# Query projection and output projection of a cached attention block: from TensorE to VectorE multiply-adds

## The chip, the cores and the metric

The kernel runs on one core of a Trainium2 chip. The metric is the device time in microseconds of one execution. The kernel before takes 1057.88 us, the median of three runs (1057.36 to 1058.01). A second number is used throughout: the span of one profiled execution, from its first instruction to its last. PE is TensorE, PEld its weight loads, DVE is VectorE, ACT is ScalarE, POOL is GpSimd, and SP is the engine whose queue issues all loads.

## The reference

One token passes through a transformer block whose keys and values are cached. Everything is fp32, the width is D = 640, and there are H = 32 heads of size 192 over 8192 cached positions.

```python
sa, ca, ga, sb, cb, gb = split6(silu(c) @ w_mod)        # w_mod: 640 x 3840
h = layernorm(x) * (1 + ca) + sa
q = (h @ wq).reshape(32 heads, 192)                      # wq: 640 x 6144
s = einsum("hd,hkd->hk", q, k_cache) * 192 ** -0.5       # k_cache: 32 x 8192 x 192
o = einsum("hk,hkd->hd", softmax(s), v_cache)            # v_cache: 32 x 8192 x 192
x = x + ga * (o.reshape(6144) @ wo)                      # wo: 6144 x 640
h = layernorm(x) * (1 + cb) + sb
x = x + gb * (relu(h @ w1 + b1) ** 2 @ w2 + b2)          # w1: 640 x 1536, w2: 1536 x 640
```

The two caches are 6144 KB a head each, 403 MB in all, and every byte is read once.

## The kernel before, in words

**Loads and slots.** Three large buffers ("slots") take turns. All loads go through SP's queue, in the order of the program: wm0 (w_mod for sa and ca, wq of the first pair, and the small vectors), k of head 0, v of head 0, k of head 1, v of head 1, and so on. A load waits on SP until the slot that it reuses is free; a load queued behind it waits too. The slot of k of a head is free when the last operation that reads it has ended (the reductions at the end of `keys`, and whatever reads the weights that came along), and it is then refilled with v of the next head. The slot of v is free when `values` has ended, and is refilled with a later k.

Heads are taken in pairs i = h // 2, and the weights of a pair ride along with k: the load of an even head brings the part of wq that makes the query of the next pair, that of an odd head the part of wo for the pair before. Heads 1 and 30 bring none. The load of k of head 30 is cut in two and that of head 31 in four pieces; the last piece of head 31 holds the rows of wo. After head 31's k come wm1 (wo of the last pair, and w_mod for ga; a second load brings sb and cb), v of head 31, w1 in two pieces, w_mod for gb, and w2 in five pieces, 3840 KB in all.

**One head.** `keys` (L192 to L208) works in place on the 64 positions of a partition, in two halves (head 31: four quarters). For each half VectorE multiplies k by the broadcast query (L201), GpSimd folds 7 of 16 parts of the products in half (L203), VectorE sums the rest (L204) and then GpSimd's share (L205). Behind the first half, `between(0)` is called: in an even head it is `query(i + 1)`, in an odd one `attend(i - 1)`. `softmax` finds the maximum over the partitions with one product of TensorE (L220) and takes the exponential on ScalarE (L228). `values` (L240) is 24 products of TensorE, 48 in the trace, which shows each fp32 product as two records. At the start of an odd head `project` (L254, L256, L258) normalises the pair before and leaves, by a product with `quad`, its outputs as columns in PSUM (ps_oT). The instructions of each engine run in the order in which the program lists them.

**query and attend.** The input h1 lies over the partitions: 4 groups of 32 lanes, and KB = 5 columns. hR is h1 with each column copied over 128 columns (L175). `query` makes five products (L181), each with a column block of hR as weights and 128 x 384 of wq as data, which add up in PSUM; ScalarE copies the sum to qb with the scale (L183). `attend` copies 96 columns of ps_oT to oT (L262), and makes six products (L267) that add up in one PSUM bank, att_a, over 15 pairs. `gather` runs in head 31 behind its third quarter's reductions: it copies att_a to SBUF and spreads it over the four groups of att (L280), to which the last pair adds its own products (L272) at the end.

**The end.** After head 31: project and attend of the last pair, the residual with ga, the second layernorm, the product with w1 (ps_f, L343), mod(5) for gb (L140), two rounds of products whose result is not used (ps_warm, L355), the product with w2 (ps_y, L363), the residual (L366, L367), and the store.

The program's order is fixed by hand: no scheduler moves instructions.

Of the kernel before, what the change touches and what calls it, by code (L numbers as in the profile page):

```python
# [20 lines left out]
DG = D // G  # L21
FG = FF // G
KB = DG // 32
FB = FG // 32
PW = 2 * DH
E = 8
ED = 64
NV = DH // ED
NPAIR = H // 2
# [16 lines left out]
def block_kernel(ctx: ExitStack, tc: tile.TileContext, kw, ky, vc, wm0, wm1, w1, gb, w2, out):  # L46
    nc = tc.nc
    const = ctx.enter_context(tc.tile_pool(name="const", bufs=1))
    strm = ctx.enter_context(tc.tile_pool(name="strm", bufs=3))
    work = ctx.enter_context(tc.tile_pool(name="work", bufs=2))  # L50
    psum = ctx.enter_context(tc.tile_pool(name="psum", bufs=1, space=bass.MemoryType.PSUM))
# [48 lines left out]
    def layernorm(x, copies, scale1, shift, name, between=lambda: None):  # L100

        n = x.shape[1]
        s = const.tile([P, 1], F32, name=name + "_s")
        nc.vector.tensor_reduce(s, x, axis=AX.X, op=ALU.add)
        m = const.tile([P, 1], F32, name=name + "_m")
        tm = total(s, name + "_tm")
        between()
        nc.vector.tensor_scalar(m, tm, 1.0 / (copies * D), None, op0=ALU.mult)
# [10 lines left out]
        nc.vector.scalar_tensor_tensor(h, xm, rs, scale1(), op0=ALU.mult, op1=ALU.mult)  # L119
        nc.vector.tensor_add(h, h, shift())  # L120
        return h
# [49 lines left out]
        return ca1  # L171

    h1 = layernorm(x_c, 1, scale_a, lambda: ma[:, :KB, 0], "ln1")
    hR = const.tile([P, KB, P], F32, name="hR")
    nc.vector.tensor_copy(hR, h1[:, :, None].to_broadcast([P, KB, P]))  # L175

    def query(i, w):
        w = w.rearrange("p (b n) -> p b n", b=KB)
        ps = psum.tile([P, 512], F32, tag="q", name=f"ps_q{i}", bufs=2)
        for b in range(KB):  # L180
            nc.tensor.matmul(ps[:, :PW], hR[:, b], w[:, b], start=(b == 0), stop=(b == KB - 1))  # L181
        qb_t[i] = work.tile([P, PW], F32, name=f"qb{i}", tag="qb")
        nc.scalar.activation(qb_t[i], ps[:, :PW], AF.Copy, scale=DH ** -0.5)  # L183


    att_a = psum.tile([P, 512], F32, tag="att", name="att_a")
# [56 lines left out]
    os_t = {}  # L243
# [14 lines left out]
        nc.tensor.matmul(os_t[i][:, :n], os_[:n].rearrange("p a d -> p (a d)"), quad[:n], start=True, stop=True)  # L258

    def attend(i, w):  # L260
        oT = work.tile([P, 96], F32, tag="oT", name=f"oT{i}")
        nc.vector.tensor_copy(oT, os_t.pop(i)[:, :96])  # L262
        w = w.rearrange("p (j n) -> p j n", j=3)
        if i + 1 < NPAIR:
            for j in range(3):
                for g in range(2):
                    nc.tensor.matmul(att_a[32 * g:32 * (g + 1), :2 * DG], oT[:, 32 * j:32 * (j + 1)],  # L267
                                     w[:, j, 2 * DG * g:2 * DG * (g + 1)], start=(i == 0 and j == 0), stop=(i == NPAIR - 2 and j == 2))
            return
        for j in range(3):  # L270
            for g in range(G):
                nc.tensor.matmul(att_t[0][32 * g:32 * (g + 1), :DG], oT[:, 32 * j:32 * (j + 1)],  # L272
                                 w[:, j, DG * g:DG * (g + 1)], start=False, stop=(j == 2))
# [67 lines left out]
    for b in range(KB):  # L341
        for g in range(G):
            nc.tensor.matmul(pf[32 * g:32 * (g + 1), :FG], hT2[:, b], w1_t[:, b, FG * g:FG * (g + 1)],  # L343
                             start=(b == 0), stop=(b == KB - 1))
    f = work.tile([P, FG], F32, name="f", tag="spread", bufs=1)
# [15 lines left out]
    for b in range(FB):  # L361
        for g in range(G):
            nc.tensor.matmul(py[32 * g:32 * (g + 1), :DG], fT[:, b], w2_t[:, b, DG * g:DG * (g + 1)],  # L363
                             start=(b == 0), stop=(b == FB - 1))
# [46 lines left out]
```

## Time and profile before

| what | value |
|---|---|
| time, median of three runs | 1057.88 us |
| span of the profiled execution | 1055.5 us |
| VectorE busy | 831.4 us (79%), 409 instructions |
| TensorE busy, matmuls | 463.7 us (44%), 2356 records |
| GpSimd busy | 194.8 us (18%) |
| ScalarE busy | 33.4 us (3%) |
| transfers of SP's queue | 451.83 MB, 99.3% of 16 engines' span |
| rate over the span | 428 GB/s |

The profiled execution has a time of its own only as this span; the medians are of other executions, and lie 2.4 us above it. A row of the timeline gives the start in the span, the duration, the engine, the line, the operation with what it writes and reads, the number of instructions, and in brackets how long the engine was idle before and what ended that. A row of the groups gives busy time and the mean duration in ns. A row of the stretches gives from and to, the length, the busy time of PE, PEld, DVE, ACT and POOL, then the granted clock of TensorE (1.00 is full), the share of the 16 transfer engines and the rate in GB/s.

### The profile page before, as it was taken

To read this page: it belongs to the slowest core of one execution; us is meant where nothing else is said; L and a number is where in the kernel's file an instruction comes from. 1 tells how busy PE (TensorE), PEld (TensorE's weight loads), DVE (VectorE), ACT (ScalarE), POOL (GpSimd) and SP (SyncE) were. 2 spreads that over 40 slices of the span, in tenths; PEclk is the share of its full clock that TensorE was granted. 3 is DMA by queue.
4 is the path that set the end of the run, shared out by engine and by line. 5 is a ranking of instruction groups with operands and counts; after the bars stand their busy time and mean duration, and the time that the engine had idled before them with its cause. 6 is when DMAs were issued, how large, how long until landed. Compare 5 with 4: busy or idle time off the path is not lost.

```text
span 1055.5 us, 5687 instructions
## 1 busy us (share of the span) xinstructions
PE 463.7 (44%) x2356; PEld 155.0 (15%) x2356; DVE 831.4 (79%) x409; ACT 33.4 (3%) x88; POOL 194.8 (18%) x72
## 2 busy tenths in 40 slices
PE   3234443355543345463334534335453335535446
PEld 1101111111111111120111111101111111111113
DVE  2886878978787987878888687997878798789963
ACT  1000000000000000000000000000000000000000
POOL 0211112211212221212221212221221221122110
PEclk9667666766666766666676666666666666767769
DMA  9999999999999999999999999999999999999997
GB/s 403 435 434 428 432 440 427 441 424 437 433 433 428 440 424 441 424 439 427 431 437 437 422 442 430 428 439 426 439 429 433 428 438 433 434 427 432 424 426 310
DMA packets 11410, 452.18 MB, mean 428 GB/s; under 512 B 1269, under 2 KB 1273, under 8 KB 1785
## 3 DMA queue, kind: packets, MB, share of 16 engines
q1 hardware_dynamic: 11384, 451.83, 99.3%
q8 instruction: 18, 0.29, 0.1%
q14 instruction: 8, 0.06, 0.0%
HBM read 451.82 MB, written 0.00 MB: 428 GB/s over the span
## 4 chain that ended last, share of the span: by engine, by line
DMA 42%; DVE 39%; PE 17%; ACT 1%; issue 1%; SPq 0%; DVEq 0%; ACTq 0%
DMA k<-in_kw 36%; DVE k L201 21%; PE ps_o L240 14%; DVE sc L204 12%; DVE sc L205 5%; DMA k<-in_ky 3%; DMA w_t<-in_w 2%; PE ps_mx L220 1%; DMA wm_t<-in_wm 1%; ACT p L228 1%; PE ps_sum L97 1%; PE ps_mod L140 1%; PE ps_q L181 1%; DVE nm L222 0%; DVE mp L218 0%
## 5 line engine op out<-in xcount | busy, mean ns | idle before, releaser
L201 DVE TENSOR_TENSOR k<-k,qb 128x6144 f32<-128x6144 f32 (+1 forms) x66 | 419.7, 6359 | 141.6 <-DMA k<-in_kw 134.4
L203 POOL TENSOR_TENSOR k<-k 128x1344 f32<-128x1344 f32 (+1 forms) x66 | 194.1, 2941 | 820.9 <-DVE k L201 476.1
L240 PE MATMUL ps_o<-v,p 128*32 128x512 f32 x1536 | 290.4, 731 | 17.2 <-ACT p L228 17.2
L204 DVE TENSOR_REDUCE sc<-k 128x18 f32<-128x3456 f32 (+1 forms) x66 | 240.5, 3644 | 4.3
L220 PE MATMUL ps_mx<-ident,mp 128*128 128x128 f32 x64 | 25.5, 501 | 416.2 <-DVE mp L218 416.2
L240 PEld LDWEIGHTS ps_o<-v,p 128*32 128x32 f32 x1536 | 68.4, 131 | 215.4 <-issue 193.1
L267 PE MATMUL att_a<-k,oT 128*32 128x320 f32 x180 | 49.6, 720 | 114.2 <-DVE oT L262 113.1
L205 DVE TENSOR_REDUCE sc<-k 128x14 f32<-128x1344 f32 (+1 forms) x66 | 99.0, 1500 | 0.0
L220 PEld LDWEIGHTS ps_mx<-ident,mp 128*128 128x128 f32 x64 | 16.1, 312 | 442.8 <-DVE mp L218 421.0
L181 PE MATMUL ps_q<-k,hR 128*128 128x384 f32 x150 | 52.3, 496 | 0.0
L228 ACT ACTIVATE p<-sc,nm 128x256 f32<-128x256 f32 x32 | 16.2, 508 | 760.6 <-DVE nm L222 496.9
L267 PEld LDWEIGHTS att_a<-k,oT 128*32 128x32 f32 x180 | 13.7, 161 | 136.7 <-DVE oT L262 116.7
L222 DVE TENSOR_REDUCE nm<-ps_mx 128x1 f32<-128x128 f32 x32 | 9.3, 291 | 28.5 <-PE ps_mx L220 28.5
L181 PEld LDWEIGHTS ps_q<-k,hR 128*128 128x128 f32 x150 | 27.3, 190 | 27.9 <-issue 11.7
L254 DVE SCALAR_TENSOR_TENSOR om<-ps_o,r,mask 96x512 f32<-96x512 f32 x32 | 23.9, 747 | 6.5 <-PE ps_o L240 5.4
L256 DVE TENSOR_REDUCE os<-om 96x64 f32<-96x512 f32 x32 | 21.8, 682 | 1.1
L140 PE MATMUL ps_mod<-wm_t,silu 128*32 128x320 f32 (+1 forms) x120 | 11.7, 550 | 14.6 <-DVE silu L128 14.6
L97 PE MATMUL ps_sum<-sp,ones 128*128 128x2 f32 x32 | 9.4, 364 | 17.2 <-ACT p L228 17.2
L183 ACT ACTIVATE qb<-ps_q 128x384 f32<-128x384 f32 x16 | 7.9, 491 | 195.2 <-PE ps_q L181 195.2
L97 PEld LDWEIGHTS ps_sum<-sp,ones 128*128 128x128 f32 x32 | 8.0, 312 | 21.9 <-ACT p L228 21.9
L145 DVE COPY mods<-ps_mod 128x320 f32<-128x320 f32 (+1 forms) x4 | 1.6, 398 | 10.2 <-PE ps_mod L140 10.2
L76 DVE COPY small<-wm_t 128x27 f32<-128x27 f32 x1 | 0.2, 179 | 11.2 <-DMA wm_t<-in_wm 11.2
(77 smaller groups left out, 90.9 us busy)
## 6 DMA issues: line engine op xcount, KB each, us to landing
k<-in_kw SPq DMA_DIRECT2D x29, 7104.0 KB, 27.4
v<-in_vc SPq DMA_DIRECT2D x32, 6144.0 KB, 22.1
k<-in_ky SPq DMA_DIRECT2D x1, 6144.0 KB, 28.3
k<-in_ky SPq DMA_DIRECT2D x2, 3072.0 KB, 21.5
k<-in_kw SPq DMA_DIRECT2D x3, 1536.0 KB, 15.5
wm_t<-in_wm SPq DMA_DIRECT2D x1, 4173.5 KB, 12.7
wm_t<-in_wm SPq DMA_DIRECT2D x1, 3200.0 KB, 29.3
wm_t<-in_wm SPq DMA_DIRECT2D x1, 2560.0 KB, 18.2
```

The source lines that it names most:

```text
L97: nc.tensor.matmul(ps[:, :n], ones, src, start=True, stop=True)
L140: nc.tensor.matmul(ps[32 * g:32 * (g + 1), :n * DG], e[:, b:b + 1].to_broadcast([P, 32]), wb[:, :, DG * g:DG * (g + 1)], start=(b == 0), s ...
L181: nc.tensor.matmul(ps[:, :PW], hR[:, b], w[:, b], start=(b == 0), stop=(b == KB - 1))
L201: nc.vector.tensor_mul(pr, pr, q[:, None, :].to_broadcast([P, n, DH]))
L203: nc.gpsimd.tensor_add(half, half, pr[:, m:, DH // 2:])
L204: nc.vector.tensor_reduce(s[:, :m], pr[:, :m], axis=AX.X, op=ALU.add)
L205: nc.vector.tensor_reduce(s[:, m:], half, axis=AX.X, op=ALU.add)
L220: nc.tensor.matmul(ps[:, :P], mp.to_broadcast([P, P]), ident, start=True, stop=True)
L228: nc.scalar.activation(p, sc[:, :, None].to_broadcast([P, NPOS, 32 // E]), AF.Exp, bias=nm, accum_out=sp[:, h % 2:h % 2 + 1])
L240: nc.tensor.matmul(ps_t[h][32 * g:32 * (g + 1)], p[:, E * j:E * (j + 1)].rearrange("p e r -> p (e r)"), t[:, j, g], start=(j == 0), stop=( ...
L254: nc.vector.scalar_tensor_tensor(om[:n], ps_t.pop(h)[:n].rearrange("p (d e) -> p d e", e=E), r2[:n, a:a + 1], mask[:n, None, :].to_broadca ...
L267: nc.tensor.matmul(att_a[32 * g:32 * (g + 1), :2 * DG], oT[:, 32 * j:32 * (j + 1)], w[:, j, 2 * DG * g:2 * DG * (g + 1)], start=(i == 0 an ...
```

## The change

`query` and `attend` use a new helper, `weighted`. It multiplies each block of a weight row by its own column scalar and adds the blocks up in SBUF, on VectorE: for wq five operations over 128 x 384 elements, for wo three over 128 x 640. What is left is a sum over the 128 partitions. For the query TensorE makes it at once, by one product with a matrix of ones. For wo the sum over 15 pairs is kept as rows in att_s, 128 x 640, and `gather` sums over the partitions once, by four products with columns of ones that put the result straight into att. oT holds three columns instead of 96 for these pairs, as one column per j is enough for a scalar. The last pair keeps its products on TensorE. hR, the bank att_a and the copy of it by ScalarE are gone. TensorE issues 154 products less (308 records). SP's loads, their order and their sizes are the same; the slots of k are read by VectorE and GpSimd only.

```diff
-    hR = const.tile([P, KB, P], F32, name="hR")
-    nc.vector.tensor_copy(hR, h1[:, :, None].to_broadcast([P, KB, P]))
+    def weighted(acc, w, by, first):
+        for j, c in enumerate(by):
+            if first and j == 0:
+                nc.vector.tensor_scalar(acc, w[:, j], c, None, op0=ALU.mult)
+            else:
+                nc.vector.scalar_tensor_tensor(acc, w[:, j], c, acc, op0=ALU.mult, op1=ALU.add)

     def query(i, w):
-        w = w.rearrange("p (b n) -> p b n", b=KB)
+        qp = work.tile([P, PW], F32, name=f"qp{i}", tag="qp", bufs=1)
+        weighted(qp, w.rearrange("p (b n) -> p b n", b=KB), [h1[:, b:b + 1] for b in range(KB)], True)
         ps = psum.tile([P, 512], F32, tag="q", name=f"ps_q{i}", bufs=2)
-        for b in range(KB):
-            nc.tensor.matmul(ps[:, :PW], hR[:, b], w[:, b], start=(b == 0), stop=(b == KB - 1))
+        nc.tensor.matmul(ps[:, :PW], ones, qp, start=True, stop=True)
...
-    att_s = const.tile([P, 2 * DG], F32, name="att_s")
-    nc.vector.memset(att_s, 0.0)
+    att_s = const.tile([P, D], F32, name="att_s")
...
         if i + 1 < NPAIR:
-            for j in range(3):
-                for g in range(2):
-                    nc.tensor.matmul(att_a[32 * g:32 * (g + 1), :2 * DG], oT[:, 32 * j:32 * (j + 1)],
-                                     w[:, j, 2 * DG * g:2 * DG * (g + 1)], start=(i == 0 and j == 0), stop=(i == NPAIR - 2 and j == 2))
+            oT = work.tile([P, NV], F32, tag="oT", name=f"oT{i}")
+            nc.vector.tensor_copy(oT, os_t.pop(i)[:, :32 * NV].rearrange("p (j r) -> p j r", j=NV)[:, :, 0])
+            weighted(att_s, w, [oT[:, j:j + 1] for j in range(NV)], i == 0)
             return
...
     def gather():
-        nc.scalar.activation(att_s[:64], att_a[:64, :2 * DG], AF.Copy)
         att_t.append(psum.tile([P, 512], F32, tag="o", name="att", bufs=3))
         for g in range(G):
-            nc.tensor.matmul(att_t[0][32 * g:32 * (g + 1), :DG], ident[:, 32 * (g // 2):32 * (g // 2) + 1].to_broadcast([P, 32]),
-                             att_s[:, DG * (g % 2):DG * (g % 2 + 1)], start=True, stop=False)
+            nc.tensor.matmul(att_t[0][32 * g:32 * (g + 1), :DG], ones[:, :32],
+                             att_s[:, DG * g:DG * (g + 1)], start=True, stop=False)
```

More of the change, by code (lines that the diff above doesn't have):

```diff
@@ L173, in block_kernel @@
     h1 = layernorm(x_c, 1, scale_a, lambda: ma[:, :KB, 0], "ln1")
-    hR = const.tile([P, KB, P], F32, name="hR")
-    nc.vector.tensor_copy(hR, h1[:, :, None].to_broadcast([P, KB, P]))
+    def weighted(acc, w, by, first):
[4 more added lines that the diff above has]
+                nc.vector.scalar_tensor_tensor(acc, w[:, j], c, acc, op0=ALU.mult, op1=ALU.add)
     def query(i, w):
-        w = w.rearrange("p (b n) -> p b n", b=KB)
+        qp = work.tile([P, PW], F32, name=f"qp{i}", tag="qp", bufs=1)
+        weighted(qp, w.rearrange("p (b n) -> p b n", b=KB), [h1[:, b:b + 1] for b in range(KB)], True)
         ps = psum.tile([P, 512], F32, tag="q", name=f"ps_q{i}", bufs=2)
-        for b in range(KB):
-            nc.tensor.matmul(ps[:, :PW], hR[:, b], w[:, b], start=(b == 0), stop=(b == KB - 1))
+        nc.tensor.matmul(ps[:, :PW], ones, qp, start=True, stop=True)
         qb_t[i] = work.tile([P, PW], F32, name=f"qb{i}", tag="qb")
         nc.scalar.activation(qb_t[i], ps[:, :PW], AF.Copy, scale=DH ** -0.5)
-    att_a = psum.tile([P, 512], F32, tag="att", name="att_a")
-    att_s = const.tile([P, 2 * DG], F32, name="att_s")
-    nc.vector.memset(att_s, 0.0)
+    att_s = const.tile([P, D], F32, name="att_s")
     att_t = []
@@ L260, in attend @@
     def attend(i, w):
-        oT = work.tile([P, 96], F32, tag="oT", name=f"oT{i}")
-        nc.vector.tensor_copy(oT, os_t.pop(i)[:, :96])
-        w = w.rearrange("p (j n) -> p j n", j=3)
+        w = w.rearrange("p (j n) -> p j n", j=NV)
         if i + 1 < NPAIR:
-            for j in range(3):
-                for g in range(2):
-                    nc.tensor.matmul(att_a[32 * g:32 * (g + 1), :2 * DG], oT[:, 32 * j:32 * (j + 1)],
-                                     w[:, j, 2 * DG * g:2 * DG * (g + 1)], start=(i == 0 and j == 0), stop=(i == NPAIR - 2 and j == 2))
+            oT = work.tile([P, NV], F32, tag="oT", name=f"oT{i}")
+            nc.vector.tensor_copy(oT, os_t.pop(i)[:, :32 * NV].rearrange("p (j r) -> p j r", j=NV)[:, :, 0])
+            weighted(att_s, w, [oT[:, j:j + 1] for j in range(NV)], i == 0)
             return
-        for j in range(3):
+        oT = work.tile([P, 32 * NV], F32, tag="oTl", name=f"oT{i}", bufs=1)
+        nc.vector.tensor_copy(oT, os_t.pop(i)[:, :32 * NV])
+        for j in range(NV):
             for g in range(G):
                 nc.tensor.matmul(att_t[0][32 * g:32 * (g + 1), :DG], oT[:, 32 * j:32 * (j + 1)],
-                                 w[:, j, DG * g:DG * (g + 1)], start=False, stop=(j == 2))
+                                 w[:, j, DG * g:DG * (g + 1)], start=False, stop=(j == NV - 1))
     def gather():
-        nc.scalar.activation(att_s[:64], att_a[:64, :2 * DG], AF.Copy)
         att_t.append(psum.tile([P, 512], F32, tag="o", name="att", bufs=3))
         for g in range(G):
-            nc.tensor.matmul(att_t[0][32 * g:32 * (g + 1), :DG], ident[:, 32 * (g // 2):32 * (g // 2) + 1].to_broadcast([P, 32]),
-                             att_s[:, DG * (g % 2):DG * (g % 2 + 1)], start=True, stop=False)
+            nc.tensor.matmul(att_t[0][32 * g:32 * (g + 1), :DG], ones[:, :32],
+                             att_s[:, DG * g:DG * (g + 1)], start=True, stop=False)
     x_t = spread(x_c, KB, "x_t")
```

## The prediction

> **What bounds the kernel now.** I read the page's queue table first, then the timeline of VectorE with what ended each idle stretch, then the chain that ended last.
>
> ```profile
> q1 hardware_dynamic: 11384, 451.83, 99.3%
> ```
>
> The transfer queue is busy for 99.3% of the span. So the body is paced by transfers, and an engine's work costs time there only when it makes a load start too late. The time must be looked for where the engines stop waiting for transfers. The timeline of VectorE (start, duration, engine, line, operation, and in brackets the idle time before and its releaser) shows where that is:
>
> ```profile
> 31.56 6.56 DVE L201 TENSOR_TENSOR k<-k,qb 128x6144 f32<-128x6144 f32 x1 [4.44 <-ACT qb L183]
> 59.33 6.56 DVE L201 TENSOR_TENSOR k<-k,qb 128x6144 f32<-128x6144 f32 x1 [2.76 <-DMA k<-in_ky]
> 908.07 6.56 DVE L201 TENSOR_TENSOR k<-k,qb 128x6144 f32<-128x6144 f32 x1 [6.12 <-DMA k<-in_kw]
> 933.20 0.75 DVE L254 SCALAR_TENSOR_TENSOR om<-ps_o,r,mask 96x512 f32<-96x512 f32 x1
> 933.99 0.68 DVE L256 TENSOR_REDUCE os<-om 96x64 f32<-96x512 f32 x1
> 939.40 6.56 DVE L201 TENSOR_TENSOR k<-k,qb 128x6144 f32<-128x6144 f32 x1 [3.24 <-DMA k<-in_kw]
> 951.20 0.25 DVE L262 COPY oT<-ps_oT 128x96 f32<-128x96 f32 x1
> 951.36 6.55 DVE L201 TENSOR_TENSOR k<-k,qb 128x6144 f32<-128x6144 f32 x1
> 999.05 0.26 DVE L262 COPY oT<-ps_oT 128x96 f32<-128x96 f32 x1 [0.38 <-PE ps_oT L258]
> ```
>
> At 59.33, 908.07 and 939.40 VectorE sits idle until a load of k lands. The idle time before an even head is 6.12 us (h=28, at 908.07) and before an odd one 3.24 us (h=29, at 939.40). 939.40 is the last such wait in the listing: from there heads 29, 30 and 31 follow one another with none. So **from 939.40 on the end is set by VectorE, and then by what follows head 31**:
>
> ```profile
> 1022.94 7.32 PE ps_o L240 x48
> ...
> 1032.07 19.60 DMA w_t<-in_w
> ...
> 1051.71 0.52 PE ps_y L363 x8
> ```
>
> The chain of waits (start, duration, what) ends with the last piece of w2. But that transfer is only just last. TensorE is working until it comes:
>
> ```profile
> 1000.16 1.81 PE L267 MATMUL att_a<-k,oT 128*32 128x320 f32 x12 [1.15 <-DMA k<-in_kw]
> 1039.47 5.13 PE L343 MATMUL ps_f<-w_t,hT 128*32 128x384 f32 x40 [2.10 <-issue]
> 1044.38 1.57 PE L140 MATMUL ps_mod<-w_t,silu 128*32 128x160 f32 x40
> 1047.46 3.16 PE L363 MATMUL ps_y<-w_t,fT 128*32 128x160 f32 x80
> ```
>
> The rows at 1039.47 to 1047.46 are ps_f, mod(5) and ps_y, with ps_warm left out between; TensorE has no gap from 1039.47 until ps_y has to wait for w2. Its weight loads show how long those waits are:
>
> ```profile
> 1049.32 0.97 PEld L363 LDWEIGHTS ps_y<-w_t,fT 128*32 128x32 f32 x32 [0.34 <-DMA w_t<-in_w]
> 1050.92 0.16 PEld L363 LDWEIGHTS ps_y<-w_t,fT 128*32 128x32 f32 x8 [0.63 <-DMA w_t<-in_w]
> 1051.71 0.16 PEld L363 LDWEIGHTS ps_y<-w_t,fT 128*32 128x32 f32 x8 [0.63 <-DMA w_t<-in_w]
> ```
>
> 0.34, 0.63 and 0.63 us, in sum 1.60: so much at most could ps_y be earlier. At least it would be as quick as mod(5), which has its shape and takes 1.57 us for 40 records: 96 take 3.77 and end at 1047.46 + 3.77 = 1051.23, against 1051.71 + 0.52 = 1052.23 now. So the compute path has 1.0 to 1.6 us of slack against the last transfer; I take 1.3, the middle. Whatever delays VectorE after 939.40 by more than that is seen in the time.
>
> **The price of an added operation.** The rows nearest to it:
>
> ```profile
> L254 DVE SCALAR_TENSOR_TENSOR om<-ps_o,r,mask 96x512 f32<-96x512 f32 x1 | 0.7, 745 | 5.4 <-PE ps_o L240 5.4
> ...
> L346 DVE TENSOR_TENSOR f<-ps_f,bbt 128x384 f32<-128x384 f32 x1 | 0.6, 558 | 5.3 <-PE ps_f L343 5.3
> ...
> L119 DVE SCALAR_TENSOR_TENSOR ln_h<-ln_xm,ln_rs,cb 128x160 f32<-128x160 f32 x1 | 0.4, 385 | 0.0
> L347 DVE TENSOR_SCALAR f<-f 128x384 f32<-128x384 f32 x1 | 0.4, 360 | 0.0
> ...
> L108 DVE TENSOR_SCALAR ln_m<-ps_ln_tm 128x1 f32<-128x1 f32 x1 | 0.2, 159 | 0.5 <-PE ps_ln_tm L97 0.5
> ```
>
> The accumulation is a scalar_tensor_tensor with a column as scalar. L119 has exactly this form (385 ns at 160 elements), L254 nearly so (745 ns at 512). Both lie on 1.04 ns an element plus 215 ns. That gives 0.615 us for 384 elements and 0.883 us for 640. Each accumulation reads the one before; such a pair, 933.20 + 0.75 to 933.99, has 0.04 us between. So one step of wo costs 0.92 us and one of wq 0.655. The first step of wq is a tensor_scalar: 0.36 us by L347, and about 0.05 more for a column in place of an immediate, 0.41.
> [...]
>
> **The change, part by part.**
> *Query, even heads.* Removed: ten TensorE records a pair, which lay beside VectorE's work. Added in front of the second half's product: 0.41 + 0.04 + 4 x 0.655 = 3.07 us, less some 0.1 by which independent neighbours overlap (951.20 + 0.25 against 951.36), 3.0. Head 28 then ends 3.0 us later and eats 3.0 of the 3.24 us before 939.40: cost nothing. If a step cost 0.1 us more, 0.2 us would run over; bound 0 to 0.5.
> *Attend, odd heads.* Removed: twelve records, beside VectorE again. The copy of oT moved VectorE on by 0.16 us (951.20 to 951.36). Now it moves three columns out of PSUM, 0.16 by L108, no overlap with what follows, and three dependent steps of 0.92 come behind it: 0.16 + 0.04 + 3 x 0.92 less 0.04 and 0.09 at their end is 2.83, minus 0.16 is 2.67 more. With tensor_tensor's price (L346 and the same slope, 0.825) it is 2.5; with gaps of 0.1 us in place of 0.04, 2.9. In the body it comes out of the 6.12 us ahead of even heads. From 939.40 it happens twice, at heads 29 and 31: 2 x 2.67 = **5.35 us on the path** (bounds 5.0 and 5.8).
> *A new wait.* The rows of wo for head 31 lie in the last of the four pieces of its load. TensorE waited for that piece (1000.16, idle 1.15 until the transfer); now VectorE would, with all of its later work behind it. But oT, which is copied at 999.05 now, is then ready at 999.05 + 2.67 + 0.16 = 1001.9, 1.7 us after the piece: nothing. If the piece landed 2 us later, 0.3.
> *gather.* Four matmuls against a column of ones instead of four against one of ident, and no copy by ScalarE: beside head 31's third quarter, nothing.
> *Start.* The spread of h1 (hR) and eight of ten records of query(0) go, five operations of VectorE come. Head 0's product waits 4.44 us for qb now (31.56); at most that is won, on a path that then waits for transfers: nothing.
> *Loads.* SP issues the load of v when k's slot is free, at the end of the head, ahead of the landing of the k before it:
>
> ```profile
> 55.14 0.33 SPq L155 DMA_DIRECT2D v<-in_vc  x1
> 931.72 0.33 SPq L155 DMA_DIRECT2D v<-in_vc  x1
> 59.33:91.75 32.42, 14.38 (x82) 4.18 (x79) 23.96 (x8) 0.60 (x2) 6.05 (x2) 0.71 1.01 437
> ```
>
> The lead is 939.40 - 931.72 = 7.7 us in the body and becomes 4.7 to 5.0. The shortest now is 59.33 - 55.14 = 4.2, and the stretch from 59.33 to 91.75 moved its bytes at 437 GB/s, with a DMA share of 1.01 (the last two numbers of its row). So leads of 4.7 cost nothing. At head 0, 4.2 loses 3.0 and wins back up to 4.44; bound 0 to 1 us once. The load of w2 is issued 5.35 us later; of the 19.60 us from issue to landing its own 3,840 KB take 9 us at the body's rate, so it stands behind 10 us of others and keeps some 5: nothing.
>
> **Sum.** 5.35 - 1.3 = 4.05 us. The profiled execution has a span of 1055.5 us, 2.4 under the median of 1057.88 us, which I take as the work around it: 1057.88 + 4.1 = **1062.0 us**, +0.4%. By bounds: 5.0 - 1.6 = 3.4 to 5.8 + 0.5 + 1 - 1.0 = 6.3.
>
> **Rivals.**
> *1. The clock of TensorE falls differently (1060.4).* The same 48 records of ps_o take between 8.42 and 9.99 us, and ps_f runs at half clock for most of its length:
>
> ```profile
> 652.21 8.42 PE L240 MATMUL ps_o<-v,p 128*32 128x512 f32 x48
> 840.21 9.99 PE L240 MATMUL ps_o<-v,p 128*32 128x512 f32 x48
> 1039.00:1040.00 1.00, 0.53 (x8) 0.34 (x12) 0.34 (x1) 0.00 (x0) 0.00 (x0) 1.00 0.97 415
> 1042.00:1043.00 1.00, 1.00 (x12) 0.54 (x8) 0.00 (x0) 0.00 (x0) 0.00 (x0) 0.50 0.93 392
> 1044.00:1045.00 1.00, 1.00 (x28) 0.84 (x24) 0.35 (x1) 0.00 (x0) 0.00 (x0) 0.95 1.03 428
> ```
>
> The granted clock (the number before the DMA share) goes from 1.00 to 0.50 in ps_f and back, within some 3.2 us. With a tail that is 5.35 us later, those stretches can fall elsewhere. If ps_f runs at full clock, 1.6 us come back: 4.05 - 1.6 = 2.45. Against it: work in the tail moves as one block, with the same gaps. The other way, ps_o of head 31 (7.32 us in the chain) takes up to 9.99 - 8.42 = 1.6 us more: 1063.6, which is in my range.
> [...]
> *2. Not slower: the accumulation runs at two elements a cycle (1059.6).* L347 does 384 elements in 360 ns where L346 takes 558. At L347's slope, 0.52 ns, 640 elements with 215 ns fixed are 0.55 us, attend adds 1.6 instead of 2.67, and 2 x 1.6 - 1.3 = 1.9 us. It decides from 0.57 us a step down, where the sum drops under 2.1 us. Against it: L119 and L254 run at 1.04 ns with this very operation.
> *3. The body loses its cover (1066 or more).* If a step of wq cost over 1 us, VectorE would pass its idle time (3.24 + 6.12 = 9.36 a pair, of which I use 5.7) and set the pace; or a lead of 4.7 us is too short and every v starts late. 0.15 us in each of 29 heads adds 4.4 us: 1066.4. Against it: the lead of 4.2 us above.
>
> **How the numbers follow.** Forecast 0.70 (its own range 1061 to 1063.8), rival 1 0.17, rival 2 0.06, rival 3 0.06, else 0.01. About 0.2%, 2.1 us, can be told from no change, so slower begins at 1060.0: slower takes the forecast, two thirds of rival 1 and rival 3, 0.87; same takes rival 2 and the rest of rival 1, 0.11; faster 0.02, as nothing on the path gets shorter by 2 us. The range 1059.8 to 1064.6 holds rival 1 and leaves out rivals 2 and 3.
>
> **What would show it.** In the profile after: L181 at 0.88 us with 640 elements and 0.62 with 384; the idle time before odd heads near 0.3 us and before even ones near 3.4; k of head 29 still landing near 939; head 31's ps_o ending 5.4 us later; ps_y with no wait for w2. The forecast is wrong if a step of wo is far from 0.9 us, if ps_f changes its clock, or if the loads of k land later from pair to pair.

## The result, and the profile after

The changed kernel takes **1065.56 us**, the median of four runs (1063.54 to 1066.62), against 1057.66 us of the kernel before beside it (1057.36 to 1058.01). The ratio is 1.0073, with a 95% interval of 1.0061 to 1.0085: slower by 7.9 us, where 4.1 were forecast. The profiled execution has a span of 1063.0 us and a time of 1064.72 us; before, the span was 1055.5 us. The executions now lie 3.1 us apart, where those of the kernel before lie 0.65 apart.

VectorE's timeline of the changed kernel, in answer to that of before:

```profile
59.43 6.56 DVE L205 TENSOR_TENSOR k<-k,qb 128x6144 f32<-128x6144 f32 x1 [1.03 <-DMA k<-in_ky]
...
93.11 6.56 DVE L205 TENSOR_TENSOR k<-k,qb 128x6144 f32<-128x6144 f32 x1 [8.73 <-DMA k<-in_kw]
...
910.74 6.56 DVE L205 TENSOR_TENSOR k<-k,qb 128x6144 f32<-128x6144 f32 x1 [3.46 <-DMA k<-in_kw]
...
942.08 6.56 DVE L205 TENSOR_TENSOR k<-k,qb 128x6144 f32<-128x6144 f32 x1 [0.30 <-DMA k<-in_kw]
...
953.88 0.15 DVE L268 COPY oT<-ps_oT 128x3 f32<-128x3 f32 x1
954.06 2.73 DVE L181 SCALAR_TENSOR_TENSOR att_s<-k,oT,att_s 128x640 f32<-128x640 f32 x3
956.71 6.55 DVE L205 TENSOR_TENSOR k<-k,qb 128x6144 f32<-128x6144 f32 x1
...
1005.75 0.16 DVE L268 COPY oT<-ps_oT 128x3 f32<-128x3 f32 x1 [1.74 <-PE ps_oT L262]
...
1008.60 3.35 DVE L205 TENSOR_TENSOR k<-k,qb 128x3072 f32<-128x3072 f32 x1
```

The added operations cost what was forecast. The three steps of wo and the copy take VectorE from 953.88 to 956.71. The idle time before head 29 is down from 3.24 to 0.30 us, that before head 28 from 6.12 to 3.46 us. But the row at 942.08 is the one that stood at 939.40: k of head 29 lands 2.68 us late. At head 2 it is already 1.36 us late (93.11; 91.75 before).

Two rows of the groups (busy time, mean ns) and the queue's row of the page:

```profile
q1 hardware_dynamic: 11384, 451.83, 98.9%
...
L181 DVE SCALAR_TENSOR_TENSOR att_s<-k,oT,att_s 128x640 f32<-128x640 f32 x44 | 38.9, 885 | 1.6
L181 DVE SCALAR_TENSOR_TENSOR qp<-k,ln_h,qp 128x384 f32<-128x384 f32 x60 | 37.1, 619 | 2.1
```

885 and 619 ns were forecast as 883 and 615. The queue is less busy, 98.9% in place of 99.3%, with the same bytes: it pauses (the pauses themselves are counted below). SP's timeline gives the issue of v of head 1 and of head 29, in answer to the rows at 55.14 and 931.72 of before:

```profile
56.93 0.33 SPq L155 DMA_DIRECT2D v<-in_vc  x1
...
937.30 0.33 SPq L155 DMA_DIRECT2D v<-in_vc  x1
```

The lead of v over the k before it is 59.43 - 56.93 = 2.5 us at head 1 (4.2 before) and 942.08 - 937.30 = 4.8 us at head 29 (7.7 before).

TensorE's timeline at the end, the weight loads of ps_y, and ps_y in the chain of waits:

```profile
995.61 9.72 PE L244 MATMUL ps_o<-v,p 128*32 128x512 f32 x48 [1.08 <-ACT p L232]
...
1032.09 8.55 PE L244 MATMUL ps_o<-v,p 128*32 128x512 f32 x48
...
1049.89 3.43 PE L345 MATMUL ps_f<-w_t,hT 128*32 128x384 f32 x40 [2.10 <-issue]
...
1056.19 3.47 PE L365 MATMUL ps_y<-w_t,fT 128*32 128x160 f32 x96
```

```profile
1056.19 3.15 PEld L365 LDWEIGHTS ps_y<-w_t,fT 128*32 128x32 f32 x92 [0.27 <-issue]
```

```profile
1056.40 3.29 PE ps_y L365 x96
```

The same products ps_o of heads 30 and 31 in TensorE's timeline of before:

```profile
990.26 8.36 PE L240 MATMUL ps_o<-v,p 128*32 128x512 f32 x48 [1.08 <-ACT p L228]
...
1022.71 7.50 PE L240 MATMUL ps_o<-v,p 128*32 128x512 f32 x48
```

ps_o of head 30 takes 9.72 us, at a mean granted clock of 0.72; before it took 8.36, at 0.84. On it waits ps_oT, and on that VectorE in head 31, for 1.74 us in place of 0.38 (row 1005.75 above). ps_o of head 31 takes 8.55 us at 0.82 (7.50 at 0.94 before), ps_f 3.43 at 1.00 (5.13 at 0.67 before). ps_y goes from 1056.19 to 1059.69 (1056.40 + 3.29), in 3.50 us where it took 4.77 (1047.46 to 1052.23): its weight loads show no wait for a transfer any more.

One stretch within ps_f, to set beside those at 1039.00 and 1042.00 of before (granted clock, DMA share and rate are the last three numbers):

```profile
1051.00:1052.00 1.00, 1.00 (x20) 0.49 (x15) 0.00 (x0) 0.00 (x0) 0.00 (x0) 1.00 1.06 415
```

TensorE runs ps_f at full clock now, 1.00 from 1049.89 to 1053.32. In sum, between the two profiled executions:

| term | forecast us | measured us |
|---|---|---|
| k of head 29 lands later (939.40, 942.08) | 0 (0 to 1) | +2.68 |
| attend in head 29 | +2.67 | +2.67 |
| VectorE in head 31 waits for ps_oT (0.38, 1.74) | 0 | +1.36 |
| attend in head 31 | +2.67 | +2.67 |
| ps_o of head 31 (7.50, 8.55) | 0 (rival 1: up to +1.6) | +1.05 |
| ps_f (5.13, 3.43) | 0 (rival 1: -1.6) | -1.70 |
| waits of ps_y for w2 (4.77, 3.50) | -1.3 | -1.27 |
| sum | +4.05 | +7.46, of 7.5 |

An attend is read from the start of one product by qb to the next: 942.08 to 956.71 is 14.63 us, 939.40 to 951.36 was 11.96.

### The profile page after: what moved, and what is told of

The parts are those of the page before. It is cut to its first block, busy times and chain, and to the rows that moved or that the text cites. A ratio compares the mean times of both kernels' runs of the same rounds, so it can differ in the third digit from the quotient of the medians.

```text
span 1063.0 us, 5178 instructions
## 1 busy us (share of the span) xinstructions
PE 384.7 (36%) x2048; PEld 119.6 (11%) x2048; DVE 913.4 (86%) x532; ACT 32.9 (3%) x87; POOL 194.8 (18%) x72
## 3 DMA queue, kind: packets, MB, share of 16 engines
q1 hardware_dynamic: 11384, 451.83, 98.9%
## 4 chain that ended last, share of the span: by engine, by line
DVE 43%; DMA 37%; PE 18%; issue 1%; ACT 1%; DVEq 0%; ACTq 0%; SPq 0%
DMA k<-in_kw 33%; DVE k L205 21%; PE ps_o L244 14%; DVE sc L208 12%; DVE sc L209 5%; DVE att_s L181 4%; DMA k<-in_ky 3%; PE ps_mx L224 1%; DMA wm_t<-in_wm 1%; PE ps_mod L140 1%; ACT p L232 1%; PE ps_sum L97 1%; DVE nm L226 0%; DVE mp L222 0%; PE ps_f L345 0%
## 5 line engine op out<-in xcount | busy, mean ns | idle before, releaser
L205 DVE TENSOR_TENSOR k<-k,qb 128x6144 f32<-128x6144 f32 (+1 forms) x66 | 419.8, 6360 | 64.5 <-DMA k<-in_kw 63.5
L244 PE MATMUL ps_o<-v,p 128*32 128x512 f32 x1536 | 295.0, 741 | 17.2 <-ACT p L232 17.2
L187 PE MATMUL ps_q<-qp,ones 128*128 128x384 f32 x32 | 26.3, 927 | 139.7 <-DVE qp L181 139.7
L181 DVE SCALAR_TENSOR_TENSOR att_s<-k,oT,att_s 128x640 f32<-128x640 f32 x44 | 38.9, 885 | 1.6
L181 DVE SCALAR_TENSOR_TENSOR qp<-k,ln_h,qp 128x384 f32<-128x384 f32 x60 | 37.1, 619 | 2.1
L187 PEld LDWEIGHTS ps_q<-qp,ones 128*128 128x128 f32 x32 | 8.0, 311 | 153.6 <-DVE qp L181 135.0
```

The lines of the kernel that those rows point to most:

```text
L181: nc.vector.scalar_tensor_tensor(acc, w[:, j], c, acc, op0=ALU.mult, op1=ALU.add)
L187: nc.tensor.matmul(ps[:, :PW], ones, qp, start=True, stop=True)
L205: nc.vector.tensor_mul(pr, pr, q[:, None, :].to_broadcast([P, n, DH]))
L244: nc.tensor.matmul(ps_t[h][32 * g:32 * (g + 1)], p[:, E * j:E * (j + 1)].rearrange("p e r -> p (e r)"), t[:, j, g], start=(j == 0), stop=( ...
```

## The experiments

Two things were not in the sum: the late stream, and the clock's share at heads 30 and 31. The theories were these. **Lead:** VectorE's work at the end of a head delays the issue of the next v, and the queue runs dry on some of its engines although the lead is still above 4 us. **Reading:** VectorE reading the weights in the slot disturbs the load into SBUF. **Clock:** the rest is the granted clock that ps_o meets.

### One part of the change alone

Query alone: `attend`, `gather` and att_a as in the kernel before. Attend alone: `query` and hR as before.

```diff
 # query alone, against the changed kernel
-            weighted(att_s, w, [oT[:, j:j + 1] for j in range(NV)], i == 0)
+            for j in range(3):
+                for g in range(2):
+                    nc.tensor.matmul(att_a[32 * g:32 * (g + 1), :2 * DG], oT[:, 32 * j:32 * (j + 1)], ...)
 # attend alone, against the changed kernel
-        nc.tensor.matmul(ps[:, :PW], ones, qp, start=True, stop=True)
+        for b in range(KB):
+            nc.tensor.matmul(ps[:, :PW], hR[:, b], w[:, b], start=(b == 0), stop=(b == KB - 1))
```

> Only query is changed; attend and gather stay on TensorE as before. Nothing is added to VectorE from head 29 on. Theory A (the shorter leads of the loads of v make the stream late): k of head 2 lands 1.3 us and k of head 29 some 2.7 us later than before (93.1 and 942.1 in the span); the slack of 1.3 us at the end takes its part, so 1057.7 + 2.7 - 1.3 = 1059.1 us. Theory B (the lateness of the stream in the profile after is chance): head 29's k lands between 939 and 941 and the time is 1057.5 to 1058.3 us.

> Only attend and gather are changed; query stays on TensorE. Theory A: no query, so head 0 keeps its lead and k of head 29 lands near 939.5; the two attends of heads 29 and 31 add 5.35 - 1.3 = 4.05 us: 1061.7 us, and up to 1.5 more or less from TensorE's clock. Theory B: the stream can be late here too, 1062 to 1065 us. In the timeline three steps of att_s take 2.7 us either way.

Query alone: 1059.98 us (1059.02 to 1064.27), ratio 1.0032 [1.0018, 1.0045]. Attend alone: 1062.64 us (1060.22 to 1066.04), ratio 1.0050 [1.0030, 1.0069]. Over the kernel before beside them, 1057.81, that is 2.2 and 4.8 us, together 7.0 of the 7.9. The query, which was forecast to cost nothing, costs 2.2 in the median and up to 6.5. The chain of its profiled execution (1063.86 us):

```profile
1039.48 18.78 DMA w_t<-in_w
...
1058.31 0.52 PE ps_y L369 x8
```

The last piece of w2 decides again, as in the kernel before, and it comes later by nearly what the stream has lost: k of head 29 lands at 946.19, 6.8 us late. The last piece lets ps_y go at 1058.31, where it was 1051.71 before: 6.6 us later. So lateness of the stream goes into the time nearly whole: w2 stands in the same stream, and the slack of 1.3 us takes none of it. That the slack would take its part was expected, and is a miss. With attend alone, k of head 29 lands at 939.53, on time, and the attend of head 29 costs 2.66; that profiled execution, with 1060.22 us, is the fastest of its five.

### The two attends behind the last wait

```diff
+LATE = (13, 14)
     def attend(i, w):
+        if i in LATE:
+            ...  # the products into att_a, as in the kernel before
+            return
```

> The changed kernel with the pairs of heads 29 and 31 (13 and 14) back on TensorE; the other 13 pairs and all queries stay on VectorE. If the two attends of the tail are 5.35 us of the path, the slack of the end comes back with them and only the late stream is left: 2.7 - 1.3 = 1.4 us over before, 1059.1 us (theory A), or 1057.5 to 1058.3 us (theory B). If the work of all pairs in the body is what costs, the time stays at 1063 us or more.

1061.75 us (1059.94 to 1063.53), ratio 1.0039 [1.0024, 1.0054]: 3.8 us less than the changed kernel, for the two attends, and still 2.7 us above what was expected. The 4 us that remain over before go with a late stream: in the profiled execution, the fastest of the four, k of head 29 lands at 942.80, 3.4 us late, and the chain ends with the last piece of w2, 2.7 us later than before (1054.38; 1051.71 before).

Then the attend's cost was added to the kernel before, in heads 29 and 31 alone. The result of the added operations is not used.

```diff
                 attend(i - 1, w)
+                if h > 28:
+                    pad()      # three steps of 128x640 on a tile of constants
```

> The kernel before with three added operations of 128x640 in heads 29 and 31 alone, behind the attend, on a tile of constants, whose result is not used (885 ns each): the attend's cost at the end, with the stream and TensorE's products as before. By the sum: 2.66 twice, less the slack of 1.3 ahead of the products with w2: +4.0, and 0 to 1.4 for the clock that the products of head 30 then meet: 1061.7 us (1060.9 to 1063.1), keys of head 29 at 939.4. If the two last heads take it up beside other work: under 1059.

1061.92 us (1061.31 to 1062.48), ratio 1.0040 [1.0026, 1.0054]: +4.3 us, where the sum gives 4.0 and the clock 0 to 1.4. VectorE's timeline of it:

```profile
939.53 6.56 DVE L210 TENSOR_TENSOR k<-k,qb 128x6144 f32<-128x6144 f32 x1 [3.25 <-DMA k<-in_kw]
...
951.49 2.72 DVE L157 SCALAR_TENSOR_TENSOR pad_s<-pad_w,ln_h,pad_s 128x640 f32<-128x640 f32 x3
954.12 6.55 DVE L210 TENSOR_TENSOR k<-k,qb 128x6144 f32<-128x6144 f32 x1
...
1003.41 0.26 DVE L271 COPY oT<-ps_oT 128x96 f32<-128x96 f32 x1 [1.98 <-PE ps_oT L267]
```

The stream is on time, the cost is there, and VectorE waits for ps_oT in this kernel too, for 1.98 us, because ps_o of head 30 takes 9.96 us here, from 993.02 on (8.36 us from 990.26 on before), though TensorE's products are those of the kernel before. So nothing need be taken from TensorE for that: here ps_o only came 2.8 us later in time.

### Where the attend stands in head 31

In head 31 the attend was put behind the second quarter, so that the late ps_oT finds VectorE at work.

```diff
-            if c == 0 and h % 2 and i:
+            if c == (1 if h == H - 1 else 0) and h % 2 and i:
                 attend(i - 1, w)
```

> The changed kernel, but in head 31 attend stands behind the second quarter instead of the first. VectorE waited 1.74 us for ps_oT there, which is queued behind ps_o of head 30 on TensorE. If that wait is on the path, it goes: 1.7 us less than the changed kernel at a slow ps_o, 0.4 at a quick one, so 1064.2 us on the mean instead of 1065.6, and a smaller spread between executions. If the wait only moves to another place, 1065.6 us.

1065.09 us (1063.59 to 1066.55), ratio 1.0069 [1.0052, 1.0086]. The wait for ps_oT is gone from the profiled execution, but k of head 29 landed at 944.84 there, and 0.5 us less in the median is inside the scatter. Inconclusive.

### TensorE's clock

Products whose result is not used were put ahead of ps_o of heads 30 and 31, to let it meet the full clock.

```diff
+            if h >= H - 2 and c in WARMED[h]:
+                for k in range(WARMED[h][c]):
+                    for g in range(G):
+                        nc.tensor.matmul(hot[32 * g:32 * (g + 1)], ones[:, :32], k_t[h][...], start=True, stop=True)
```

> The changed kernel with idle products on TensorE, whose results are not used, before the softmax of heads 30 and 31, so that ps_o of both heads meets a full clock. Theory C (the clock of TensorE is part of the loss): ps_o of head 30 takes about 7 us instead of 9.7 and that of head 31 about 7 instead of 8.4; the wait of VectorE for ps_oT in head 31 falls from 1.7 us to nothing; 1065.6 - 1.4 - 1.5 = 1062.7 us. Without theory C the time stays at 1065.6 us.

1062.91 us (1060.66 to 1065.55), ratio 1.0046 [1.0029, 1.0063]: 2.65 us less than the changed kernel. TensorE's and VectorE's timelines of the profiled execution, which is the slowest of the four:

```profile
999.91 7.07 PE L250 MATMUL ps_o<-v,p 128*32 128x512 f32 x48 [1.08 <-ACT p L238]
...
1032.93 7.04 PE L250 MATMUL ps_o<-v,p 128*32 128x512 f32 x48
```

```profile
1008.60 2.73 DVE L182 SCALAR_TENSOR_TENSOR att_s<-k,oT,att_s 128x640 f32<-128x640 f32 x3 [0.21 <-DMA k<-in_kw]
```

ps_o takes 7.07 and 7.04 us where it took 9.72 and 8.55. On the path lie VectorE's wait of 1.74 us and the 1.51 of head 31, so 3.25 at most. VectorE no longer waits for ps_oT, but for the last piece of k of head 31, 0.21 us, the wait named in the prediction. Here the stream is 7.3 us late (k of head 29 at 946.70), which hides part of the gain. From that landing to the end of ps_y it is 113.8 us here (946.70 to 1060.50), and 117.6 in the changed kernel (942.08 to 1059.66). So in these two traces the clock is seen to cost time at the end; that the median falls by it rests on four executions of each kernel, whose ranges overlap. Its share in the changed kernel is about 2.4 us in one execution (1.36 + 1.05), against 1.7 won by ps_f.

### Is it the reading of the weights, or the lead?

The kernel before got five operations of the query's form and size behind its query in even heads. They read a tile of constants, and their result is not used.

```diff
                 query(i + 1, w)
+                pad()
```

> The kernel before, with five operations on VectorE added to each even head where query stands, of the size and form that the changed query has, but on a tile of ones that is no part of a slot; their result is not used. All queries and attends stay on TensorE. Theory L (VectorE's 3 us end keys later, the load of v is issued with a lead of 4.7 us in place of 7.7, and the transfer engines that run ahead go dry): k of head 29 lands 2 to 7 us late, and the time is that of the query alone, 1059 to 1064 us, with the same spread. Theory R (it is the reading of the weights by VectorE that disturbs the transfers): k of head 29 lands at 939 to 940 and the time is 1057.8 us.

1061.98 us (1059.51 to 1064.88), ratio 1.0047 [1.0031, 1.0064]. k of head 2 lands at 92.97 and k of head 29 at 943.96. Nothing reads the weights more than before, and TensorE's products are all there: **the reading is refuted, the lead stands.**

Then the early loss at head 2 was taken out: only the query of pair 1 went back to TensorE, and hR is built behind the first query.

```diff
     def query(i, w):
+        if i == 1:
+            ...  # the five products with hR, as in the kernel before
+            return
```

> The changed kernel with the query of pair 1 alone on TensorE, so that head 0 ends 3 us earlier and the load of v of head 1 has a lead of 5.4 us instead of 2.5. Theory L: k of head 2 lands at 91.8 to 92.1 instead of 93.1; 1.0 to 1.3 us are won on the path: 1064.4 us. If the first loads don't matter, 1065.6 us.

k of head 2 landed at 91.67, on time. The time is 1064.0 us (1063.0 to 1067.01), ratio 1.0068 [1.0051, 1.0084], 1.6 us less than the changed kernel with ranges that overlap; in the profiled execution, the slowest, k of head 29 is 4.9 us late all the same. So the loss at head 2 is no special case of the start. It comes again later.

### What a lead of 4.7 us lacks

The trace has, for every load, the moments at which the 16 transfer engines end their shares of it. From these: the lead of a v (from its issue to the landing of the k before) as the first and as the last of the engines see it, the pause of the first (its time for the load over the 14.53 us that 6144 KB take, 16.80 for 7104), and the spread from first to last landing.

```
kernel          load         lead to last  lead to first  pause of first  spread
before          v of head 1      4.17          3.34           0.00          1.83
before          v of head 17     7.61          5.46           0.00          3.20
before          v of head 29     7.59          3.99           0.00          3.61
changed         v of head 1      2.47          1.55           0.83          2.35
changed         v of head 15     4.65          2.26           0.28          2.11
changed         v of head 24     4.81          2.39           0.58          1.94
pad of five     v of head 7      4.61          1.07           0.85          2.86

over the loads 5 to 60 of 14 kernels, by the lead to the first landing:
lead to first   loads   mean pause   largest
under 1.2          6       1.12        1.50
1.2 to 1.6        11       0.53        1.04
1.6 to 2.0        17       0.55        1.00
2.0 to 2.4        50       0.31        0.89
2.4 to 2.8        76       0.11        0.61
2.8 to 3.2        42       0.05        0.41
3.2 to 4.0        25       0.00        0.05
over 4.0         557      -0.01        0.12
```

The 16 engines do not land together. In the kernel before, the spread grows from 0.8 to 3.6 us over the heads, in four steps of 0.3 to 1.1 us, at the last landings of 74.84, 325.81, 577.55 and 828.55. During each of these four loads the trace has a fetch of instructions, 16 KB each, at 61.9, 312.9, 564.6 and 817.5. The queues' part of the stretch from 61.5 to 63.5 us (packets, MB, share of 16 engines) shows the first:

```profile
q1 hardware_dynamic: 18, 0.88, 103.8%
q8 instruction: 1, 0.02, 3.0%
```

3.0% of 16 engines for 2 us is 0.96 us of one engine. Of the 14 fetches in the body ten leave the last landing in its place to within 0.1 us; by the theory they meet an engine that is ahead. By it too, the engines that are not hit run ahead, by as much as the spread, and need the next load so much earlier. In the table a pause begins where the first of them has less than about 3 us between issue and its own landing of the load before (0.11 us on the mean at a lead of 2.4 to 2.8, 0.05 at 2.8 to 3.2). With 7.7 us of lead and a spread of up to 3.6, 4 us are left. With 4.7, some 2.3 are left, and the pauses take back what the leading engines had won (the spread goes from 2.35 to 1.38 us between v of head 1 and v of head 9 of the changed kernel); by the theory a later hit then falls on all.

What a short lead costs is not the same in every execution: with attend alone every second lead in the body falls to about 4.8 us, the first engine pauses three times (0.9 us in all), and k of head 29 is still on time in the execution that was profiled. If the engine that a fetch meets differs from execution to execution, which no run shows, the scatter follows too: 1059.0 to 1064.3 us with the query alone, 1.1 us over 27 executions of the kernel before.

In the kernel before, the packets in the trace show what a fetch does: at each of the 14, 16 packets of loads are under way just before and just after it, and 15 in its middle. So each fetch takes its 0.97 to 1.10 us from the share of one engine. That these hits add up to the spread is argued from there: no run took the fetches away, and the engines were not followed one by one from load to load. What the runs show is the lead's part: the table here, and the pads, which add nothing but work of VectorE ahead of the release of a slot.

A load is there for VectorE only when the last of its 16 engines has landed: k of head 29 in the kernel before has landings from 935.71 to 939.31, and VectorE starts on it at 939.40. From the second load of v on, the spreads in the traces are 1.4 to 4.2 us.

Two parts of the 3 us can be read from the packets. The first load of the program meets an idle queue: in the 14 traces its first packet starts 1.0 us after its issue, and the last of the 16 engines starts on it after 1.6 to 2.6 us. And an engine's landing stands in the trace some 0.3 to 0.6 us after the end of its last packet. Together that is 1.3 to 3.2 us, an estimate of the lead that an engine needs if it is not to pause, and the table's edge lies at its upper end.

By the table and the spread, 2 us less of lead than 7.7 would cost something, 1 us nothing. The pad was cut to two of its five operations:

```diff
-        for j in range(KB):
+        for j in range(2):
```

> The kernel before with two added operations of the query's form and size on a tile of constants in every even head, whose result is not used (about 1.03 us instead of the 2.9 of the run with five). The lead goes from 7.7 to 6.7 us. Theory of the lead, by which it must cover the spread of the landings (up to 3.6) and some 2.6 us for the engine furthest ahead, 6.2 together: no lateness, keys of head 29 at 939.4 to 940.0, time 1057.6 us (1057.0 to 1058.4). If the lateness grows in proportion to the time that the v is issued later: a third of the 4.3 us that five operations cost, 1059.1.

1057.63 us (1057.03 to 1060.01, eleven runs), ratio 1.0002 [0.9993, 1.0011]; k of head 29 lands at 939.31, and the first engine does not pause. Not a third of 4.3 us, but nothing in the median; two of the eleven, at 1059.36 and 1060.01, are higher than any of the 27 of the kernel before beside them (1057.02 to 1058.16), so 6.7 us is near the edge.

### The added work in another place

If only the place of the work is wrong, it can go where VectorE is idle: ahead of the keys of a head, where it waits for k. ScalarE copies the rows of wq out of the slot, which frees k as before, and VectorE works on the copy at the start of the next odd head.

```diff
             elif c == 0 and h % 2 == 0 and i + 1 < NPAIR:
-                query(i + 1, w)
+                nc.scalar.activation(wq_s, w, AF.Copy)
+                aside[i + 1] = wq_s
...
+        if h % 2 and i + 1 in aside:
+            query(i + 1, aside.pop(i + 1))
         sc = keys(h, between)
```

> The changed kernel, but ScalarE copies the rows of wq aside in the even head and VectorE works on the copy in the next odd head, ahead of its keys, where it waits for the load of k. The same work on VectorE, and keys of the even head ends 3 us earlier again. Theory L: the lead is 7.7 us, k of head 29 lands at 939 to 940, and what is left is the two attends less the slack: 1057.8 + 5.35 - 1.3 = 1061.9 us, with up to 1.5 us either way from the clock. If the work and not its place makes the stream late, k of head 29 lands past 942 and the time is 1065 us.

> The query's rows of wq set aside by ScalarE and summed by VectorE in the next odd head ahead of its keys, and the attends of pairs 13 and 14 back on TensorE: the two failed steps undone together, 13 of 15 attends and all queries still on VectorE. If they add up: the last v is late as in the run with the deferred query alone (keys of head 29 at 940.0 to 943, 939.4 before), and the end is the last transfer of w2 again, so the time is before's 1057.6 plus that lateness: 1059.2 us (1058.2 to 1061.5). If the late attends cost nothing of their own: 1062.6, as with the deferred query alone.

With the query deferred: 1062.65 us (1060.76 to 1064.15), ratio 1.0049 [1.0034, 1.0064], k of head 29 at 940.90. With pairs 13 and 14 back on TensorE besides: **1058.12 us** (1056.55 to 1060.26), ratio 1.0007 [0.9998, 1.0017]. What the two undo adds up, to within 0.5 us of before and just under the range that was expected. A rest of lateness is left (940.98) in the profiled execution, and four loads with pauses; in odd heads the attends still lie ahead of the last product, and shorten the lead of the next v to about 4.8.

So the rows of wo were set aside too, for pairs 0 to 12, and worked on at the start of the next even head.

```diff
-            weighted(att_s, w, [oT[:, j:j + 1] for j in range(NV)], i == 0)
+            nc.scalar.activation(wo_s, w.rearrange("p j n -> p (j n)"), AF.Copy)
+            later.append((i, oT, wo_s.rearrange("p (j n) -> p j n", j=NV)))
...
+        if h % 2 == 0 and later:
+            k, oT, wo_s = later.pop()
+            weighted(att_s, wo_s, [oT[:, j:j + 1] for j in range(NV)], k == 0)
```

> As the run before this one, and the rows of wo of pairs 0 to 12 are set aside by ScalarE too and summed by VectorE in the next even head ahead of its keys. In no head does VectorE then work on weights between the scores of the first quarter and the last of the keys, so the lead of the next v over the k before it stays at about 7.7 us in every head, and the added work lies in the idle time ahead of the keys (3.2 us before odd heads, 6.1 before even ones). Theory of the lead: keys of head 2 at 91.7, of head 29 at 939.4 to 940.0, no engine that is ahead goes dry, time that of before within 0.2%: 1057.6 us (1057.0 to 1058.6), and the executions agree to about 1 us again. If it is VectorE's added 80 us as such, or its reading of the weights' tile, that make the stream late: over 1059.5, with a spread of 3 us or more.

**1056.77 us** (1056.53 to 1057.26, eleven runs), ratio 0.9992 [0.9984, 1.0001]. VectorE's timeline, and the page's first lines:

```profile
902.20 2.72 DVE L182 SCALAR_TENSOR_TENSOR att_s<-wo_s,oT,att_s 128x640 f32<-128x640 f32 x3
908.51 6.56 DVE L209 TENSOR_TENSOR k<-k,qb 128x6144 f32<-128x6144 f32 x1 [3.60 <-DMA k<-in_kw]
...
936.90 2.58 DVE L182 SCALAR_TENSOR_TENSOR qp<-wq_s,ln_h,qp 128x384 f32<-128x384 f32 x4
939.92 6.56 DVE L209 TENSOR_TENSOR k<-k,qb 128x6144 f32<-128x6144 f32 x1 [0.44 <-DMA k<-in_kw]
```

```profile
PE 374.8 (36%) x2080; PEld 116.9 (11%) x2080; DVE 907.0 (86%) x527; ACT 82.4 (8%) x116; POOL 194.7 (18%) x72
...
q1 hardware_dynamic: 11384, 451.83, 99.4%
```

VectorE does all of the queries and 13 of the 15 attends, and is busy for 86% of the span as in the changed kernel; TensorE has fewer products than before, the idle time before head 29 is 0.44 us, and it costs nothing: no pause of the first engine over 0.11 us (0.12 in the kernel before), the queue at 99.4%, and executions that agree to 0.7 us. Whether it is faster than the kernel before by the 0.85 us between the medians can't be told from this interval.

## Why the prediction was wrong, point by point

- **Where the time is set.** Right. From the landing of k of head 29 on, VectorE's work is on the path; before it, it counts only through the start of loads.
- **Prices.** Right: 885 and 619 ns (883 and 615 forecast), 2.67 us for each of the two attends, idle times of 0.30 and 3.46 us (0.3 and 3.4). The first step of wq, forecast as 0.41 us with 0.05 of it an estimate for the column, takes 411 ns (L179; L349 with an immediate 360). Rival 2 needed a step of wo at 0.57 us or less and is out at 0.885: the accumulation takes 1.04 ns an element (885 and 619 ns), not the 0.52 of L347 and L108; how many elements a cycle that is, no run shows.
- **Slack.** The size was right (1.27 for 1.3), its reach was not: it helps against work of VectorE behind 939.40, and not against a late stream, because w2 is late with it.
- **"So leads of 4.7 cost nothing."** This is the step that failed, and rival 3 in its second half ("a lead of 4.7 us is too short") had the mechanism, at a chance of 0.06. Two readings were wrong. The lead was taken to the landing of k, which is that of the last engine; the first, 2 to 4 us ahead, is the one that runs dry (pauses of 0.28 to 0.83 us in the table's rows of the changed kernel). And the proof, a lead of 4.2 us at head 1 with a full stretch of 437 GB/s behind it, came from a place where the engines are still together (lead to the first 3.34 us). It cost 2.68 us in the profiled execution, 2.2 in the median with the query alone.
- **The start's bound of 0 to 1 us.** Measured 1.36 at head 2, and no special case: with it taken away the stream was late further on.
- **The clock.** Rival 1 had the right rows, and both of its directions came at once: ps_f won 1.70, ps_o of head 31 lost 1.05. What was missing is a third place: ps_o of head 30 is on the path through ps_oT, on which VectorE already waited 0.38 us (the row at 999.05), and grew by 1.36. A product that already had a wait of VectorE behind it has no cover. The net was +0.7.
- **The new wait for head 31's last piece of k.** It stayed away in the changed kernel and came, with 0.21 us, where ps_o was quick and the stream late.
- **Head 31's load of w2**, said to keep some 5 us: in the changed kernel ps_y meets no wait for it. Right, for a stream that is 2.7 us late.

The forecast of 0.70 for +4.05 is what the attends in heads 29 and 31 alone cost (+4.3). Of the other 3.6 us the query alone accounts for 2.2, through the lead. The 1.4 that are left were not separated; the attends of the body shorten leads too, and attend alone is 0.7 us over the run with the cost in heads 29 and 31 alone (1062.64, 1061.92).

## What to carry to other kernels

In a kernel that is bound by a stream of loads, idle time of an engine is not all free: work that stands ahead of the release of a buffer shortens the lead of the next load (here five operations in every even head, 2.9 us, took it from 7.7 to 4.7 us and cost 4.3 us), and the same work ahead of the wait for data costs nothing (here 1056.77 us against 1057.62, with all queries and 13 of 15 attends moved there). Measure the lead to the first of the transfer engines to finish, not to the landing of the load, and leave room for their spread; a scatter between executions that grows, here from 1 to 5 us, is a sign that it no longer does. Behind the last wait for the stream, add up the new work at its full price, with every product of another engine that was only just in time.

## What was not expected of the hardware

The 16 engines that share every load drift apart by up to 3.6 us over the heads of the kernel before and by 4.2 in the one with both parts deferred, and in these traces they come together again where the first of them pauses (2.35 to 1.38 us from head 1 to head 9 of the changed kernel). The same 48 products of ps_o take 7.04 to 9.99 us by TensorE's granted clock: in the kernel before 7.50 us at a mean of 0.94, 8.42 at 0.83 and 9.99 at 0.70, 7.0 us in each case if time and clock are multiplied. With unused products ahead of them they took 7.07 and 7.04; in head 31 of the run with the attend behind the second quarter they took 7.04 without. What sets the granted clock no run shows. Between the medians with and without the unused products lie 2.65 us of 1065.56, 0.25%, with ranges that overlap. That is two thirds of the forecast change all the same.
